# Gated mix of linear attention and a dilated local window: first tiles interleaved, warm-up on a constant, last columns split evenly

## The chip, the cores and the metric

The kernel runs on one core of a Trainium2 chip. The time is the device time of one execution in microseconds (us). The engines are TensorE (PE; its weight loads are shown as PEld), VectorE (DVE), ScalarE (ACT), GpSimd (POOL) and SyncE (SP), which issues most of the DMA transfers. A row named SPq or ACTq is the issue of a transfer on that engine's queue.

## The reference

```python
x = A_x                                    # [1, 2048, 1024] bf16
g = sigmoid((x * gate_w).sum(-1, keepdims=True))
# A: linear attention, 32 heads of 32
q, k, v = split(x @ A_wqkv)
pq, pk = phi(q), phi(k)                    # phi(t) = where(t > 0, t + 1, exp(t)) + 1e-6
kv = einsum("bhsd,bhse->bhde", pk, v);  z = einsum("bhsd->bhd", pk)
a = ((pq @ kv) / (pq . z + 1e-6)) @ A_wo
# B: each token attends to 8 keys, itself and every second token before it
q, k, v = split(x @ B_wqkv)
b = (softmax(q . k_window * 32**-0.5, masked at the start) @ v_window) @ B_wo
return g * a + (1 - g) * b                 # B_x is not used
```

## The kernel before

Activations are held transposed in `xT`: eight chunks of 128 features on the partitions, 2048 tokens along the free side. They arrive by 16 DMA transposes of 128 tokens each (`load_x`, line 1315). Even and odd tokens are separated, so a window of stride 2 becomes a run of neighbours. Weights arrive by `load_w` (line 1320) into slots of 1024 columns, in halves of 512 columns.

The stages stand one after the other on TensorE. (1) A warm-up: `WARM` small matmuls whose result is not used. (2) The values of B: for each block of four token tiles, half 0 and then half 1 of the 1024 value columns; every tile and half is one accumulation group of eight 128x512 matmuls (`group`, line 1340), copied out of PSUM by ACT or DVE (`move`, lines 1367 and 1368) into a ring `vst` and stored to `vB_hbm` (line 1389). (3) Keys and queries of B, with the window attention (`fill`) interleaved. (4) Keys of A, state, values and the fold of the output weights. (5) Queries of A and the output: for each tile two column ranges of 512, each the sum of 16 matmuls (line 1681), scaled by `gm` (line 1370) and stored (line 1688). The last tile is cut into (0, 512), (512, 896) and (896, 1024).

No engine's order is written by hand: `Prog.schedule` runs a list scheduler over all operations with estimated costs and priorities, chooses ACT or DVE for each `move`, and repeats the plan with PSUM banks chosen by when they were free in the plan before. What each engine executes is its own list in that order, with semaphore waits between the lists. Each queue issues its transfers in order.

For the first tiles this gives the following. On SP: x0, two pieces of the first weight half (chunks 4-5 and 6-7), x1, x2, x3, four pieces of the second half, then stores and x4 to x15. On ACT: the two other pieces of the first half (chunks 0-1 and 2-3), then the load of its function table. In the text these pieces are w0 to w3 (first half) and w4 to w7 (second half), and x0 to x15 are the token tiles. TensorE takes tile 0 in steps of two chunks, so that it waits for one weight piece at a time, and the other tiles in steps of eight:

```python
for t, half in [(4 * b + i, half) for b in range(NT // 4) for half in range(2) for i in range(4)]:
    ...
    step = 2 if t == 0 else 8
    for d in range(0, 8, step):
        o = group(bank, xs, w, [xr, ws[0].part((d, d + step), ...)], d, d + step)
```

The warm-up reads a tile `warm` that DVE sets to zero (line 1293). The same tile is used later for other purposes.

Of the kernel before, what the change touches and what calls it, by code (L numbers as in the profile page):

```python
# [9 lines left out]
BF16 = mybir.dt.bfloat16  # L10
# [1106 lines left out]
def build_kernel(nc, A_x, A_wqkv, A_wo, B_x, B_wqkv, B_wo, gate_w, out):  # L1117
    del B_x
    S = A_x.shape[1]
    NT = S // 128  # L1120
# [7 lines left out]
    def SB(shape, dtype, name, at=None):  # L1128
        n = SZ[dtype]
        for d in shape[1:]:  # L1130
            n *= d
        if at is None:
            at = base[0]
            base[0] += (n + 31) // 32 * 32
        uid[0] += 1
        h = nc.alloc_sbuf_tensor_at("%s_%d" % (name, uid[0]), list(shape), dtype, offset=at)
        return Tile("S", h, at, list(shape), dtype)
# [41 lines left out]
    banks = [Bank(i) for i in range(8)]  # L1179
# [4 lines left out]
    def hb(p0, p1, half):  # L1184
        return [("H%d" % half, p0, p1, None)]
# [4 lines left out]
    ws = [SB([128, 8, 1024], BF16, "w%d" % i) for i in range(4)]  # L1190
# [20 lines left out]
    warm = SB([128, 512], BF16, "warm")  # L1211
# [29 lines left out]
    FILL = 0.2  # L1241
    PVLAG = 3
    SUMS_AT = 2
    WARM = 46
    PASSES = 6
    mm = lambda n: max(n / 2400.0, 0.0267) + 0.0025
    act = lambda n: 0.19 + n / 1200.0
    dps = lambda n: 0.14 + n / 960.0

    def plan(seen):  # L1250

        P = Prog(nc, nc.alloc_semaphore)
# [23 lines left out]
        def C(eng, fn, cost, writes, reads=()):  # L1276
            return P.op(eng, fn, cost, reads=reads, writes=writes, prio=-1)
# [35 lines left out]
        def load_x(t, prio):  # L1313
            e_, r = t // 8, t % 8
            return P.op("sp", lambda e: e.dma_start_transpose(xT[:, :, t * 128:(t + 1) * 128], x2[e_, r * 128:(r + 1) * 128, :]),  # L1315
                        1.5, writes=[xT.part((0, 8), (t * 128, (t + 1) * 128))], prio=prio, chan="x%d" % t, lat=1.3)

        def load_w(slot, half, src, c0, prio, d0=0, d1=8, eng="sp", after=()):
            n = d1 - d0
            return P.op(eng, lambda e: e.dma_start(ws[slot][:, d0:d1, half * 512:half * 512 + 512], src[:, d0:d1, c0:c0 + 512]), 0.4 + 0.2 * n,  # L1320
                        writes=[ws[slot].part((d0, d1), (half * 512, half * 512 + 512))], prio=prio, chan="w%d_%d_%d" % (slot, half, d0), lat=0.55 * n, after=after)

        load_x(0, 0)
        load_w(0, 0, Bw, 2048, 0.1, 0, 2, "act")
        load_w(0, 0, Bw, 2048, 0.2, 2, 4, "act")
        load_w(0, 0, Bw, 2048, 0.3, 4, 6)
        load_w(0, 0, Bw, 2048, 0.4, 6, 8)
        for t in range(1, NT):
            load_x(t, 3 + t)
        for d in range(0, 8, 2):  # L1330
            load_w(0, 1, Bw, 2560, 6.1 + 0.1 * d, d, d + 2)
# [2 lines left out]
        main = Pool(banks[0:7])  # L1334

        def group(bank, lhs, rhs, reads, lo=0, hi=8):
            def fn(e):
                last = None
                for dc in range(lo, hi):
                    last = e.matmul(bank.ap(), lhs(dc), rhs(dc), start=(dc == 0), stop=(dc == 7))  # L1340
                return last
            return P.op("pe", fn, (hi - lo) * mm(512), reads=reads, writes=[bank.iv])
# [9 lines left out]
        def x_tile(t):  # L1352
            return (lambda dc: xT[:, dc, t * 128:(t + 1) * 128]), xT.part((0, 8), (t * 128, (t + 1) * 128))

        def x_chunk(u):
            return (lambda dc: xT[:, dc, u * 512:(u + 1) * 512]), xT.part((0, 8), (u * 512, (u + 1) * 512))

        def w_half(slot, half):
            return (lambda dc: ws[slot][:, dc, half * 512:half * 512 + 512]), ws[slot].part((0, 8), (half * 512, half * 512 + 512))

        def w_cols(slot, j):
            return (lambda dc: ws[slot][:, dc, j * 128:(j + 1) * 128]), ws[slot].part((0, 8), (j * 128, (j + 1) * 128))

        def move(dst, src, n, bank, reg, scale=None, reads=()):

            if scale is None:
                fd = lambda e: e.tensor_copy(dst, src())  # L1367
                fa = lambda e: e.activation(dst, src(), ACT.Copy)  # L1368
            else:
                fd = lambda e: e.tensor_scalar(dst, src(), scale, None, op0=ALU.mult)  # L1370
                fa = lambda e: e.activation(dst, src(), ACT.Copy, scale=scale)
            P.op("any", {"act": fa, "dve": fd}, {"act": act(n) + (0.1 if reads else 0.0), "dve": dps(n)}, reads=[bank.iv] + list(reads), writes=[reg])

        for i in range(WARM):
            P.op("pe", lambda e: e.matmul(banks[7].ap(0, 156), warm[:, 0:128], warm[:, 0:156], start=True, stop=True), 0.13, reads=[warm.all()], writes=[banks[7].iv], prio=-1)


        early = {(2, 0): (1, 0, Bw, 1024, 21), (4, 1): (2, 0, Bw, 0, 22), (7, 1): (1, 1, Bw, 1536, 23), (10, 1): (2, 1, Bw, 512, 24),
                 (12, 1): (3, 0, Aw, 1024, 25), (14, 1): (3, 1, Aw, 1536, 26)}
        for t, half in [(4 * b + i, half) for b in range(NT // 4) for half in range(2) for i in range(4)]:  # L1380
            vt, vs = vst.next()
            xs, xr = x_tile(t)
            bank = main.next()
            w, wr = w_half(0, half)
            step = 2 if t == 0 else 8
            for d in range(0, 8, step):
                o = group(bank, xs, w, [xr, ws[0].part((d, d + step), (half * 512, half * 512 + 512))], d, d + step)
            move(vt[:, :], bank.ap, 512, bank, vt.all())
            P.op("sp", lambda e, t=t, vt=vt, half=half: e.dma_start(vB_hbm[t * 128:(t + 1) * 128, half * 512:half * 512 + 512], vt[:, :]), 0.6, reads=[vt.all()],
                 writes=[hb(t * 128, (t + 1) * 128, half)], chan="vst%d" % vs, lat=0.5, prio=5)  # L1390
            if (t, half) in early:
                load_w(*early[t, half], after=[o])
# [14 lines left out]
        main = Pool(banks[0:4])  # L1407
# [77 lines left out]
        for e_ in range(2):  # L1485
            if True:
                for j in range(8):
                    for isq in range(2):
                        for u in (2 * e_, 2 * e_ + 1):
                            bank = main.next()  # L1490
                            w, wr = w_cols(1 + isq, j)
                            xs, xr = x_chunk(u)
# [45 lines left out]
        for t in range(NT):  # L1538
            xs, xr = x_tile(t)
            for r in range(2):  # L1540
                bank = main.next()
                w, wr = w_half(3, r)
                o = group(bank, xs, w, [xr, wr])
# [33 lines left out]
        main = Pool(banks[0:3])  # L1577
# [23 lines left out]
        for c in range(8):  # L1601
            tl = xns[c // 2]
            cs = (c % 2) * 128
            for r in range(2):
                bank = main.next()
# [63 lines left out]
        def output(t):  # L1669
            o_, os_ = osb.next()  # L1670
            e_, r = t // 8, t % 8
            parts = [(0, 512), (512, 1024)] if t < NT - 1 else [(0, 512), (512, 896), (896, 1024)]
            for f0, f1 in parts:
                bank = main.next()
                n = f1 - f0

                tt = (t * 128, (t + 1) * 128)
                for lh, w, first in ((qT, ws[0], True), (aT, ws[5], False)):
                    def fn(e, bank=bank, f0=f0, f1=f1, lh=lh, w=w, first=first):
                        for k in range(8):  # L1680
                            last = e.matmul(bank.ap(0, f1 - f0), lh[:, k, t * 128:(t + 1) * 128], w[:, k, f0:f1], start=(first and k == 0), stop=(not first and k == 7))  # L1681
                        return last
                    P.op("pe", fn, 8 * mm(n), reads=[lh.part((0, 8), tt), w.part((0, 8), (f0, f1))], writes=[bank.iv])
                move(o_[:, f0:f1], lambda bank=bank, n=n: bank.ap(0, n), n, bank, o_.part((f0, f1)), gm[:, t:t + 1], [gm.all()])
                P.ops[-1].late = t == NT - 1
                if t == NT - 1 or f1 == 1024:
                    c = f0 if t == NT - 1 else 0
                    P.op("sp", lambda e, c=c, f1=f1: e.dma_start(out2[e_, r * 128:(r + 1) * 128, c:f1], o_[:, c:f1]), 0.5,
                         reads=[o_.part((c, f1))], chan="out%d_%d" % (os_ + 2 * (t == NT - 1), c), lat=1.0, name="out")
                    P.ops[-1].late = t == NT - 1  # L1690
# [10 lines left out]
        main = Pool(banks)  # L1701
# [17 lines left out]
        for t in range(NT):  # L1719
            if t + 2 < NT:  # L1720
                scaled(t + 2)
            output(t)
            if t + 5 < NT:
                queries(t + 5)

        C("act", lambda e: e.preload_act_table_set("natural_log_exp_and_others"), 1.3, [])
        P.ops[-1].prio = 2.5
        P.schedule()
        return P, flag_op, [max(o.end for o in P.held[n]) for n in range(len(takes))]

# [2 lines left out]
    for _ in range(PASSES):  # L1733
        got = plan(seen)
        seen = got[2]
        if best is None or got[0].span < best[0].span:
            best = got
    P, flag_op = best[:2]
# [40 lines left out]
def bass_gated_mix__linear_attn_block__sliding_local_dilated__prompt_kernel(nc, A_x, A_wqkv, A_wo, B_x, B_wqkv, B_wo, gate_w, out):  # L1779
    return build_kernel(nc, A_x, A_wqkv, A_wo, B_x, B_wqkv, B_wo, gate_w, out)  # L1780
# [28 lines left out]
```

## Time and profile before

| | |
|---|---|
| median of 3 runs | 489.4 us (488.79 to 491.67) |
| the profiled execution | 488.05 us, its span 486.3 us |
| granted TensorE clock, mean | 1.000 |
| busy: PE, DVE, ACT, POOL | 474.2, 290.3, 148.1, 40.9 us |
| moved by DMA | 47.72 MB, mean 98 GB/s |

The span runs from the first to the last instruction of the core. Busy time of an engine counts its instructions; a matmul's row includes its way through the array, so rows of one stream overlap. Queue rows give the time of the issue; the landing of a transfer is given apart, from issue to the last byte. An entry in brackets at the end of a row is the idle time of the engine before it and what ended it.

### The profile page before, as it was taken

The page shows a single profiled execution, that of the slowest core. Times are in us where ns is not written, and L with a number is a line of the kernel's source. Part 1 is how long each engine was busy: PE and PEld are TensorE (multiplying, and loading weights), DVE is VectorE, ACT ScalarE, POOL GpSimd, SP SyncE. Part 2 cuts the span into 40 slices and gives each one's busy share as a digit, 9 for nine tenths or more (in the row PEclk, how much of TensorE's full clock was granted, in tenths as well). Part 3 has the DMA queues.
Part 4 walks back from the last instruction along what each step waited for, and adds up shares of the span by engine and source line. Part 5 has one row for each costly group of instructions (what it writes and reads, how often), then busy time and mean ns, then how long its engine had stood idle before and what let it go on. Part 6 is the DMA issues. An engine that isn't in the chain of part 4 may idle for free.

```text
span 486.3 us, 10903 instructions
## 1 busy us (share of the span) xinstructions
PE 474.2 (97%) x4820; PEld 228.6 (47%) x4883; DVE 290.3 (60%) x486; ACT 148.1 (30%) x231; POOL 40.9 (8%) x43
## 2 busy tenths in 40 slices
PE   8999999999999999999999999999999999999997
PEld 6444444444444444444455545444444444444443
DVE  2121455899777777766733222289987777767522
ACT  2111121112344444766554356544222000011000
POOL 3000000000000000000025657100000000000000
PEclk9999999999999999999999999999999999999999
DMA  8999997224000032213004430252233111122111
GB/s 223 205 204 281 341 332 232 86 88 129 3 23 25 27 115 58 35 34 111 24 25 121 141 91 4 89 174 41 54 80 87 44 43 44 44 71 60 44 44 48
DMA packets 71833, 47.72 MB, mean 98 GB/s; under 512 B 36449, under 2 KB 65378, under 8 KB 71778
## 3 DMA queue, kind: packets, MB, share of 16 engines
q1 hardware_dynamic: 71234, 46.42, 34.7%
q8 instruction: 40, 0.66, 0.6%
q10 hardware_dynamic: 544, 0.52, 0.4%
q14 instruction: 15, 0.12, 0.1%
HBM read 30.15 MB, written 8.39 MB: 79 GB/s over the span
## 4 chain that ended last, share of the span: by engine, by line
PE 94%; SPq 2%; issue 2%; DMA 1%; DVE 0%; ACT 0%
PE ps_all L1340 54%; PE ps_all L1681 23%; PE ps_all L1609 11%; PE ps_all L1426 2%; PE ps_all L1446 2%; SPq L1315 1%; DMA w<-in_B_wqkv_dram 1%; PE ps_all L1452 1%; SPq L1320 1%; PE ps_all L1588 1%; PE ps_all L1636 0%; DVE qT L1463 0%; ACT L L1461 0%; PE ps_all L1558 0%; ACT L L1462 0%
## 5 line engine op out<-in xcount | busy, mean ns | idle before, releaser
L1340 PE MATMUL ps_all<-w,xT 128*128 128x512 bf16 x493 | 109.9, 379 | 2.6 <-issue 2.1
L1340 PE MATMUL ps_all<-xT,w 128*128 128x512 bf16 x498 | 109.9, 379 | 1.7 <-issue 1.4
L1340 PEld LDWEIGHTS ps_all<-xT,w 128*128 128x128 bf16 x512 | 49.4, 98 | 58.6
L1340 PEld LDWEIGHTS ps_all<-w,xT 128*128 128x128 bf16 x512 | 48.8, 98 | 58.3 <-DMA w<-in_B_wqkv_dram 0.7
L1346 ACT ACTIVATE e<-ps_all 128x512 bf16<-128x512 f32 x64 | 38.0, 598 | 109.7 <-PE ps_all L1340 107.9
L1681 PE MATMUL ps_all<-kT,aT 128*128 128x512 bf16 (+2 forms) x261 | 60.3, 373 | 0.2
L1681 PE MATMUL ps_all<-w,qT 128*128 128x512 bf16 (+2 forms) x259 | 60.2, 372 | 0.3
L1340 PE MATMUL ps_all<-kT,xT 128*128 128x512 bf16 x248 | 57.1, 379 | 0.6 <-issue 0.3
L1609 PE MATMUL ps_all<-pk,xn 128*128 128x512 bf16 x243 | 54.9, 379 | 2.0 <-issue 1.9
L1681 PEld LDWEIGHTS ps_all<-w,qT 128*128 128x128 bf16 x264 | 25.6, 98 | 30.0
L1681 PEld LDWEIGHTS ps_all<-kT,aT 128*128 128x128 bf16 x264 | 25.4, 98 | 29.8 <-issue 0.2
L1340 PEld LDWEIGHTS ps_all<-kT,xT 128*128 128x128 bf16 x256 | 24.7, 98 | 30.0 <-issue 0.5
L1463 DVE TENSOR_TENSOR qT<-ps_all,L 128x456 bf16<-128x456 f32 (+1 forms) x36 | 21.1, 625 | 27.6 <-ACT L L1462 27.6
L1609 PEld LDWEIGHTS ps_all<-pk,xn 128*128 128x128 bf16 x256 | 24.1, 98 | 27.6
L1367 DVE CAST vst<-ps_all 128x512 bf16<-128x512 f32 x15 | 10.4, 692 | 44.4 <-PE ps_all L1340 44.4
L1370 DVE TENSOR_SCALAR o<-ps_all,gm 128x512 bf16<-128x512 f32 (+2 forms) x27 | 19.7, 731 | 28.0 <-PE ps_all L1681 28.0
L1435 DVE TENSOR_TENSOR E<-E,msk 128x1824 bf16<-128x1824 bf16 (+1 forms) x18 | 20.4, 1133 | 26.5 <-ACT E L1432 26.5
L1432 ACT ACTIVATE E<-ps_all 128x1824 bf16<-128x1824 f32 (+1 forms) x18 | 30.4, 1688 | 14.3 <-PE ps_all L1426 13.6
L1347 DVE TENSOR_SCALAR e<-e 128x512 bf16<-128x512 bf16 x64 | 18.4, 288 | 27.2 <-ACT e L1346 27.2
L1571 POOL TENSOR_TENSOR zacc<-zacc,pk 128x1024 f32<-128x1024 f32 x15 | 31.9, 2130 | 16.6 <-DVE E L1435 15.8
L1301 DVE TENSOR_TENSOR mx<-mx,kT 128x1024 bf16<-128x1024 bf16 x32 | 20.8, 686 | 6.9 <-ACT kT L1368 6.8
L1368 ACT ACTIVATE vst<-ps_all 128x512 bf16<-128x512 f32 x17 | 10.2, 597 | 48.0 <-PE ps_all L1340 45.1
(67 smaller groups left out, 354.4 us busy)
## 6 DMA issues: line engine op xcount, KB each, us to landing
v<-vB_hbm SPq DMA_DIRECT2D x36, 128.0 KB, 2.7
vB_hbm<-vst SPq DMA_DIRECT2D x32, 128.0 KB, 6.1
w<-in_B_wqkv_dram SPq DMA_DIRECT2D x4, 1024.0 KB, 8.7
xt<-in_A_x_dram SPq DMA_DIRECT2D x16, 256.0 KB, 4.9
w<-in_A_wqkv_dram SPq DMA_DIRECT2D x4, 1024.0 KB, 10.1
xn<-in_A_x_dram SPq DMA_DIRECT2D x8, 512.0 KB, 3.7
out_dram<-o SPq DMA_DIRECT2D x15, 256.0 KB, 2.1
kT<-in_A_wqkv_dram SPq DMA_DIRECT2D x2, 1024.0 KB, 5.6
```

The costliest lines, as they stand in the source:

```text
L1301: P.op("dve", lambda e, m=m, op=op: e.tensor_tensor(m[:, 0:n], m[:, 0:n], src, op), 0.08 + n / 1920.0, reads=[m.all(), reg], writes=[m.all()],
L1340: last = e.matmul(bank.ap(), lhs(dc), rhs(dc), start=(dc == 0), stop=(dc == 7))
L1346: P.op("act", lambda e: e.activation(e_[:, :], bank.ap(), ACT.Exp), act(512), reads=[bank.iv], writes=[e_.all()])
L1347: P.op("dve", lambda e: e.tensor_scalar(e_[:, :], e_[:, :], 1.0, 1e-6, op0=ALU.min, op1=ALU.add), 0.25, reads=[e_.all()], writes=[e_.all()])
L1367: fd = lambda e: e.tensor_copy(dst, src())
L1370: fd = lambda e: e.tensor_scalar(dst, src(), scale, None, op0=ALU.mult)
L1432: P.op("act", lambda e: e.activation(E[:, 0:32 * nq].rearrange("p (j q) -> p j q", j=4), ps[:, 4:8, 0:8 * nq], ACT.Exp), act(32 * nq), rea ...
L1435: mk = P.op("dve", lambda e: e.tensor_tensor(ev(), ev(), m[:, :, :].rearrange("p r q -> p (r q)")[:, None, :].to_broadcast([128, 16, 2 * n ...
L1463: P.op("dve", lambda e, L=L, pb=pb, g=g: e.tensor_tensor(qT[:, 4 * g:4 * g + 4, t0 + qs:t0 + qs + 2 * nq].rearrange("p c (h q) -> p h c q" ...
L1571: P.op("pool", lambda e, t=t: e.tensor_tensor(zacc[:, :], zacc[:, :], pkS[:, t, :], ALU.add), 2.2, reads=[src, zacc.all()], writes=[zacc.a ...
L1609: last = e.matmul(bank.ap(), tl[:, t, cs:cs + 128], pkS[:, t, r * 512:(r + 1) * 512], start=(t == 0), stop=(t == NT - 1))
L1681: last = e.matmul(bank.ap(0, f1 - f0), lh[:, k, t * 128:(t + 1) * 128], w[:, k, f0:f1], start=(first and k == 0), stop=(not first and k == 7))
```

## The change

- `WARM` goes from 46 to 34, and the warm-up matmuls read a constant 1.0 that the framework keeps in SBUF (broadcast over 128 and 156 columns) in place of the tile `warm`; they wait for nothing.
- ACT's table load is put at the head of ACT's list, ahead of its two weight pieces. Before it stood behind them.
- x1 is issued directly after x0, ahead of SP's two pieces of the first half.
- In the first block, tiles 0 and 1 are interleaved by weight piece: in half 0 four chunks of tile 0, four of tile 1, then two and two, two and two; in half 1 two and two for each of the four pieces. Two accumulation groups are open in two PSUM banks. Tiles 2 and 3 and the other blocks are as before.
- The last tile's second half is cut into 256 and 256 columns in place of 384 and 128.

```diff
-    WARM = 46
+    WARM = 34
...
+        P.op("act", lambda e: e.preload_act_table_set("natural_log_exp_and_others"), 1.3, [], prio=-1)
         load_x(0, 0)
+        load_x(1, 0.1)
         load_w(0, 0, Bw, 2048, 0.1, 0, 2, "act")
         load_w(0, 0, Bw, 2048, 0.2, 2, 4, "act")
         load_w(0, 0, Bw, 2048, 0.3, 4, 6)
         load_w(0, 0, Bw, 2048, 0.4, 6, 8)
-        for t in range(1, NT):
+        for t in range(2, NT):
             load_x(t, 3 + t)
...
+        one = lambda n: nc.const_aps.tensor(1.0, [128, n], BF16)
         for i in range(WARM):
-            P.op("pe", lambda e: e.matmul(banks[7].ap(0, 156), warm[:, 0:128], warm[:, 0:156], start=True, stop=True), 0.13, reads=[warm.all()], writes=[banks[7].iv], prio=-1)
+            P.op("pe", lambda e: e.matmul(banks[7].ap(0, 156), one(128), one(156), start=True, stop=True), 0.13, writes=[banks[7].iv], prio=-1)
...
-        for t, half in [(4 * b + i, half) for b in range(NT // 4) for half in range(2) for i in range(4)]:
+        steps = []
+        for b in range(NT // 4):
+            for half in range(2):
+                if b == 0:
+                    cuts = [(0, 4), (4, 6), (6, 8)] if half == 0 else [(0, 2), (2, 4), (4, 6), (6, 8)]
+                    steps += [[(i, half, lo, hi) for i in range(2)] for lo, hi in cuts]
+                    steps += [[(2, half, 0, 8)], [(3, half, 0, 8)]]
+                else:
+                    steps += [[(4 * b + i, half, 0, 8)] for i in range(4)]
+        open_ = {}
+        for t, half, lo, hi in [p for q in steps for p in q]:
+            xs, xr = x_tile(t)
+            if lo == 0:
+                open_[t, half] = main.next()
+            bank = open_[t, half]
+            w, wr = w_half(0, half)
+            o = group(bank, xs, w, [xr, ws[0].part((lo, hi), (half * 512, half * 512 + 512))], lo, hi)
+            if hi < 8:
+                continue
             vt, vs = vst.next()
-            xs, xr = x_tile(t)
-            bank = main.next()
-            w, wr = w_half(0, half)
-            step = 2 if t == 0 else 8
-            for d in range(0, 8, step):
-                o = group(bank, xs, w, [xr, ws[0].part((d, d + step), (half * 512, half * 512 + 512))], d, d + step)
             move(vt[:, :], bank.ap, 512, bank, vt.all())
...
-            parts = [(0, 512), (512, 1024)] if t < NT - 1 else [(0, 512), (512, 896), (896, 1024)]
+            parts = [(0, 512), (512, 1024)] if t < NT - 1 else [(0, 512), (512, 768), (768, 1024)]
...
-        C("act", lambda e: e.preload_act_table_set("natural_log_exp_and_others"), 1.3, [])
-        P.ops[-1].prio = 2.5
```

## The prediction

> **What bounds the kernel now.** First I read the page's busy shares and its chain of work that ended last:
>
> ```profile
> PE 474.2 (97%) x4820; PEld 228.6 (47%) x4883; DVE 290.3 (60%) x486; ACT 148.1 (30%) x231; POOL 40.9 (8%) x43
> ...
> PE 94%; SPq 2%; issue 2%; DMA 1%; DVE 0%; ACT 0%
> ```
>
> TensorE is busy for 97% of the span and carries 94% of the chain, so only an edit that moves TensorE's first matmul, a hole between its matmuls, or the few microseconds after its last one can move the end. The change touches the first stretch and the last. The timeline of the first (start, length, engine, line; then idle time and what ended it):
>
> ```profile
> 0.80 0.94 ACTq L1320 DMA_DIRECT2D w<-in_B_wqkv_dram  x2
> 0.80 1.35 SPq L1315 DMA_TRANSPOSE xT<-in_A_x_dram  x1
> ...
> 0.93 0.27 DVE L1293 MEMSET warm<- 128x256 uint32 x1 [0.93 <-PEq L1794]
> 1.25 5.26 PE L1375 MATMUL ps_all<-warm 128*128 128x156 bf16 x46 [1.25 <-DVE warm L1293]
> 1.77 1.28 ACT L1726 ACT_TABLE_LOAD   x1 [1.77 <-PEq L1794]
> 2.21 1.07 SPq L1320 DMA_DIRECT2D w<-in_B_wqkv_dram  x2
> 3.33 4.98 SPq L1315 DMA_TRANSPOSE xT<-in_A_x_dram  x3
> 6.35 8.45 PE L1340 MATMUL ps_all<-w,xT 128*128 128x512 bf16 x37
> 8.15 6.16 PEld L1340 LDWEIGHTS ps_all<-w,xT 128*128 128x128 bf16 x30 [0.40 <-DMA xT<-in_A_x_dram]
> 15.06 30.18 PE L1340 MATMUL ps_all<-w,xT 128*128 128x512 bf16 x136 [0.26 <-DMA w<-in_B_wqkv_dram]
> ...
> 19.33 1.23 SPq L1315 DMA_TRANSPOSE xT<-in_A_x_dram  x1
> ```
>
> The 46 warm-up matmuls wait for a memset (0.93 to 1.20) and run from 1.25 to 6.51 with the tails of the last ones; real work starts at 6.35. The weight loader waits once for a transposed token tile (8.15, 0.40 us), and TensorE once for a weight piece (15.06, with 0.26 us of idle shown). That hole is larger than it looks, since a matmul's row includes its pipeline. Eight 512-column matmuls follow one another in 477.69 − 475.96 = 1.73 us (rows in the tail below), so one takes 0.216 us. In program order 38 matmuls stand before the one that waits at 15.06: four tiles of 8 in the first half, then six of tile 0's second half. From 6.35 they would need 38 × 0.216 = 8.21 us, to 14.56; so 0.50 us is lost in all. I use an "effective start": the time at which an unbroken stream would have begun to be where it is after the last hole. Now it is 15.06 − 8.21 = **6.85**. After that the row shows 30 us without a wait.
>
> When do the data land? The view of a tile's transfers gives issue time and issue-to-landing, for x0, then x1, x2 and all sixteen; for the weight pieces w0 and w1 together (ACT's queue), w2 and w3 together (SP's); and the chain for the last piece of the second half, w7:
>
> ```profile
> L1315 SPq DMA_TRANSPOSE xT<-in_A_x_dram x1: 1350/1350/1350, 0.8 to 0.8; - x1
> DMA to landing us min/median/max: 5.1/5.1/5.1
> ...
> L1315 SPq DMA_TRANSPOSE xT<-in_A_x_dram x1: 1239/1239/1239, 3.3 to 3.3; - x1
> DMA to landing us min/median/max: 4.8/4.8/4.8
> ...
> L1315 SPq DMA_TRANSPOSE xT<-in_A_x_dram x1: 2348/2348/2348, 4.6 to 4.6; - x1
> DMA to landing us min/median/max: 4.6/4.6/4.6
> ...
> L1315 SPq DMA_TRANSPOSE xT<-in_A_x_dram x16: 1231/1284/2436, 0.8 to 35.8; - x16
> ...
> DMA to landing us min/median/max: 3.3/3.9/5.9
> ```
>
> ```profile
> L1320 ACTq DMA_DIRECT2D w<-in_B_wqkv_dram x2: 423/456/488, 0.8 to 1.3; - x2
> DMA to landing us min/median/max: 2.8/3.6/4.4
> ...
> L1320 SPq DMA_DIRECT2D w<-in_B_wqkv_dram x2: 457/510/562, 2.2 to 2.8; - x2
> DMA to landing us min/median/max: 4.4/4.4/4.5
> ```
>
> ```profile
> 10.00 5.01 DMA w<-in_B_wqkv_dram
> ```
>
> So x0 lands at 0.80 + 5.1 = 5.9, w1 at 1.3 + 4.4 = 5.7, w2 and w3 at 2.2 + 4.4 = 6.6 and 2.8 + 4.5 = 7.3, x1 at 3.3 + 4.8 = 8.1, x2 at 4.6 + 4.6 = 9.2, w7 at 15.0. Landings follow the order of issue.
>
> **The change, part by part.** *Second tile's load up, tiles interleaved.* SP now issues x0, x1, w2, w3, x2, x3, then w4 to w7 and x4: the same six issues stand ahead of x2, so x2 and what follows keep their times. x1's issue takes 1.24 us (4.98 for three in the row, the first starting at 3.33, x2 at 4.6), so x1 moves from 3.3 to about 2.2, and w2, w3 from 2.2, 2.8 to about 3.5, 4.1. TensorE does four matmuls of tile 0 (which now wait for x0, w0 and w1 together), four of tile 1, then two and two for w2, two and two for w3, tiles 2 and 3 whole; in the second half two and two per piece. Each arrival sets a lower bound on the effective start, landing minus matmuls ahead × 0.216:
>
> x0 5.9 − 0 = 5.9. w1 5.7 − 0 = 5.7. x1 (2.2 + 5.0, between the 5.1 and 4.8 of x0 and x1) 7.2 − 4 × 0.216 = 6.35. w2 3.5 + 4.4 = 7.9 − 8 × 0.216 = 6.2. w3 4.1 + 4.5 = 8.6 − 12 × 0.216 = 6.0. x2 9.2 − 16 × 0.216 = 5.75. w7 15.0 − 44 × 0.216 = 5.5.
>
> The largest is x1's, 6.35, so 6.85 − 6.35 = **0.5 us gained**. The hole at w7 goes because six more matmuls stand before it (44, not 38); what is late next is x1, a hole of about 0.4 us after the first four matmuls. Bounds: if x1, w2 and w3 land sooner than issue times say, x0 at 5.9 remains, a gain of 0.95; if x1 still lands at 8.1, the start is 8.1 − 0.86 = 7.24, a loss of 0.4.
>
> *Table load first.* ACT now begins with the table load (1.28 us at 1.77) and only then issues w0 and w1, which tile 0 waits for; x0 and x1 are behind SP and not touched. The trace never shows a DMA issue behind a running ACT instruction, so the cost is bounded by 0 (the issue goes out while the table loads) and 1.28 us (it waits). In the second case w1 lands at 5.7 + 1.28 = 7.0, and the start is 7.0 instead of 6.35, 0.65 us worse. I take 0: issue (ACTq) and execution (ACT) are separate rows in this view, and of the two ends nothing shows the second. On ACT's own side the load is covered, since the first eviction comes after 8 us.
>
> *Warm-ups: 34 on a constant.* The constant is set before the engines enter the block, so they start near 0.8 (where ACT and SP start), 0.45 us sooner, and are 12 fewer. The record of the warm-ups, and two windows of 0.2 us (PE busy and matmuls in flight come first, the granted clock third from the end):
>
> ```profile
> L1375 PE MATMUL ps_all<-warm x46: 228/336/336, 1.3 to 6.3; 128*128 128x156 bf16 x46
> ```
>
> ```profile
> 5.00:5.20 0.20, 0.20 (x4) 0.20 (x3) 0.00 (x0) 0.00 (x0) 0.20 (x2) 1.00 1.28 366
> 6.00:6.20 0.20, 0.20 (x6) 0.20 (x4) 0.00 (x0) 0.00 (x0) 0.00 (x0) 1.00 1.16 369
> ```
>
> With lengths from 336 to 228 ns and 4 then 6 in flight per 0.2 us window, spacing goes from (0.336 + 0.2) / 4 = 0.134 to (0.228 + 0.2) / 6 = 0.071 us between 5.2 and 6.0, though the granted clock reads 1.00 in both. About 4.2 us of continuous work came before the faster rate. Thirty-four at the slow rate take 4.56 us, to about 5.4, just past that point (0.8 + 4.2 = 5.0); then TensorE idles until 5.9. I charge nothing: both the twelve removed and the earlier end lie ahead of x0's landing. If that cover fails, because the faster rate has not come by then, every real matmul costs 0.216 × 0.134 / 0.071 = 0.41 instead of 0.216 us until it does (second rival).
>
> The Trainium skill, "TensorE: Matmul & The Clock Gate" (Part 1: The HAM clock gate), says that the array runs at half rate until one busy window of about 3.4 us has passed, and that this window runs freely, so the moment shifts from run to run. The 4.2 us above agrees with it; by that rule, as an estimate, a stretch of 4.56 us need not hold a whole window, which speaks against the shorter warm-up.
>
> *Other orders.* Many evictions of the first 100 us change between ACT and DVE, and the queues of stores and token loads are reshuffled. TensorE's own order after the first four tiles is unchanged. The cover is the distance of the loads: x7 is issued at 19.33 with 13 loads and 4 stores ahead, as many as after the change; it lands within 5.9 us, by 25.2 at worst and by the median 3.9 at 23.2, and is needed after 88 matmuls, 6.35 + 19.0 = 25.35. Without that cover each microsecond late is one lost. I take 0.
>
> *Last columns 256 and 256.*
>
> ```profile
> 475.96 1.89 PE L1681 MATMUL ps_all<-w,qT 128*128 128x512 bf16 x8
> 477.69 1.89 PE L1681 MATMUL ps_all<-kT,aT 128*128 128x512 bf16 x8
> 479.41 1.46 PE L1681 MATMUL ps_all<-w,qT 128*128 128x384 bf16 x8
> 482.01 0.61 PE L1681 MATMUL ps_all<-w,qT 128*128 128x128 bf16 x8
> 482.22 0.62 DVE L1370 TENSOR_SCALAR o<-ps_all,gm 128x384 bf16<-128x384 f32 x1 [1.61 <-PE ps_all L1681]
> 482.46 0.61 PE L1681 MATMUL ps_all<-kT,aT 128*128 128x128 bf16 x8
> ```
>
> ```profile
> 482.86 1.84 SPq L1688 DMA_DIRECT2D out_dram<-o  x2
> 483.11 0.35 DVE L1370 TENSOR_SCALAR o<-ps_all,gm 128x128 bf16<-128x128 f32 x1 [0.28 <-PE ps_all L1681]
> ```
>
> ```profile
> out_dram<-o SPq DMA_DIRECT2D x1, 128.0 KB, 1.7
> out_dram<-o SPq DMA_DIRECT2D x1, 96.0 KB, 2.6
> out_dram<-o SPq DMA_DIRECT2D x1, 32.0 KB, 2.3
> ```
>
> Sixteen matmuls of 384 columns take 482.01 − 479.41 = 2.60 us, sixteen of 128 take 2 × 0.45 = 0.90; 256 lies midway, 32 × 0.109 = 3.5, no change. A matmul's own length is its eight's less seven spacings: 1.46 − 7 × 0.1625 = 0.32 at 384 columns, 0.61 − 7 × 0.056 = 0.22 at 128, so the last one at 256 ends some 0.05 later. The last eviction goes from 0.35 to the mean of 0.35 and 0.62, +0.135. The last store, issued now when the eviction ends (483.46) and landing 2.3 later at 485.8, is issued 0.19 us later. A store of 64 KB isn't in the trace: 2.6 for 96 KB, 2.3 for 32, 1.7 for 128. I take 2.0, between its neighbour in size below and the best, since its predecessor is now over a microsecond away instead of 0.6. Sum +0.19 − 0.3 = **−0.1 us**, bounds −0.4 and +0.5.
>
> The Trainium skill, "DMA: Bandwidth & Descriptors" (Specifications), puts the least size for line rate at 512 B; rows of 128 columns are 256 B, rows of 256 are 512 B. That would favour 1.7, though the 96 KB store with 768 B rows took 2.6 here.
>
> **Sum.** −0.5 − 0.1 = −0.6 us on the profiled execution's 488.05 (span 486.3 and 1.75 around it), 487.45. The runs' median of 489.4 is 1.35 above that execution; on that footing the forecast is **488.8 us**, a gain of 0.1%. One per cent (4.9 us) is about what a measurement of this kernel can tell from no change.
>
> **Rivals.** *The table load holds w0 and w1* (the change doesn't start sooner as it says). Effective start 7.0 against 6.85: +0.15 − 0.1, 489.45. For it: one queue, in order. Against: separate rows for issue and execution.
>
> *Slower: the real matmuls begin at the slow rate.* Place: the gap between the last warm-up (5.4) and x0 (5.9). It decides when the faster rate has not come by 5.4; then another 4.2 us at 0.41 us hold about 10 matmuls instead of 19. Started at 5.9, ten are done at 10.1, an effective start of 10.1 − 2.16 = 7.95, +1.1 − 0.1: 490.4. With w1 held too it starts at 7.0 and reaches 9.05: 491.5. For it: 4.56 us of warm-up is hardly more than the 4.2 that it took. Against: the gap is short, and the rate rose before the end here. The clock-gate section of the Trainium skill's page "TensorE: Matmul & The Clock Gate" describes this mechanism.
>
> *All six first transfers land together.* If moving x1 only reorders one saturated stream, x1 lands at 8.1: 7.24, +0.4 − 0.1, 489.7. For it: the same bytes move in the same time. Against: landings followed issue.
>
> **How the numbers follow.** Forecast 0.5, held queue 0.18, slow rate 0.2, together 0.12. The range starts from the best bounds, 489.4 − 0.95 − 0.4 = 488.05, less 1.25 because a median can come out like the profiled execution (1.35 lower): 486.8. Above, it reaches 491.2, through the slow-rate case and most of its worse form. The forecast's own range is 487.4 to 489.9. Every case lies within 1% of 489.4; I leave 0.03 each side for late loads and stray effects.
>
> **What would show it.** Right: warm-ups from 0.8 ending near 5.2; the first real matmul near 5.9; a wait for x1 after four of them; no hole at a second-half weight piece; tile 4 about 0.5 us sooner; the last store landing 2.0 us or less after its issue. Wrong: ACTq issues at 2.1; real matmuls 0.41 us apart after 6; a hole at x5 to x7; a difference over 2 us anywhere else.

## The result and the profile after

The changed kernel took 488.03 us (median of 22 runs, 486.66 to 490.36); the kernel before took 489.81 us beside it (22 runs, 488.55 to 493.31). The ratio is 0.9962, with a 95% interval of 0.9948 to 0.9976: 1.9 us faster, at least 1.2 and at most 2.5. The profiled execution took 487.48 us with a span of 485.7 us, 0.57 and 0.6 us less than the profiled execution before. So the profiled pair shows the 0.6 us that was forecast, while the medians show three times as much. In a second comparison the ratio was 0.9975 (0.9954 to 0.9996).

The page after, busy shares and the chain that ended last:

```profile
PE 473.4 (97%) x4808; PEld 228.6 (47%) x4871; DVE 291.0 (60%) x487; ACT 147.4 (30%) x230; POOL 40.8 (8%) x43
...
PE 96%; issue 2%; DMA 1%; DVE 0%; ACT 0%
```

TensorE's share is as before. In the chain it has gone from 94% to 96%, because the transfers and issues that stood in it at the start have left it. The timeline of the start shows why:

```profile
0.80 1.28 ACT L1323 ACT_TABLE_LOAD   x1 [0.80 <-PEq L1807]
0.80 2.71 SPq L1315 DMA_TRANSPOSE xT<-in_A_x_dram  x2
...
0.83 0.96 ACTq L1320 DMA_DIRECT2D w<-in_B_wqkv_dram  x2
0.84 4.58 PE L1378 MATMUL ps_all<-const-bfloat16-1.0 128*128 128x156 bf16 x34 [0.84 <-PEq L1807]
...
3.57 1.09 SPq L1320 DMA_DIRECT2D w<-in_B_wqkv_dram  x2
...
6.09 24.08 PE L1342 MATMUL ps_all<-w,xT 128*128 128x512 bf16 x108 [0.67 <-DMA xT<-in_A_x_dram]
```

Four things are to be seen. ACT issues its two weight pieces (ACTq, 0.83) while the table load runs (0.80 to 2.08). The 34 warm-up matmuls start at 0.84, last to 5.42 and are followed by 0.67 us of idle time, ended by x0. The first real matmul starts at 6.09, and there is no further wait in the row: neither at x1 nor at a second-half piece. x1's landing is the other number (issue and landing of x0 and x1 together):

```profile
L1315 SPq DMA_TRANSPOSE xT<-in_A_x_dram x2: 1309/1330/1350, 0.8 to 2.2; - x2
DMA to landing us min/median/max: 4.3/4.7/5.2
```

x1 was issued at 2.2 and landed 4.3 us later, at 6.5, not 7.2. What this start is worth is read at a point behind it in the same order of TensorE, the first matmuls of the first window attention. Their row before, and after:

```profile
126.10 0.70 PE L1426 MATMUL ps_all<-qT,kT 32*64 32x57 bf16 x64
```

```profile
125.50 0.70 PE L1441 MATMUL ps_all<-qT,kT 32*64 32x57 bf16 x64
```

That is 0.60 us sooner. The end of the span, with the last two evictions and the last store:

```profile
481.14 0.48 DVE L1372 TENSOR_SCALAR o<-ps_all,gm 128x256 bf16<-128x256 f32 x1 [0.50 <-PE ps_all L1696]
...
482.88 0.48 DVE L1372 TENSOR_SCALAR o<-ps_all,gm 128x256 bf16<-128x256 f32 x1 [1.26 <-PE ps_all L1696]
```

```profile
L1703 SPq DMA_DIRECT2D out_dram<-o x1: 332/332/332, 483.4 to 483.4; - x1
DMA to landing us min/median/max: 1.8/1.8/1.8
```

The last eviction starts 0.23 us sooner than before (483.11), the store lands 1.8 us after its issue where it took 2.3, and the span ends 2.82 us after that eviction began, where it ended 3.19 us after it, 0.37 us less. Between the start and the tail, 0.37 us was given back at one place, near 195 us. The `E,v` rows are matmuls of the attention's second half; the rows behind them (ACT's logarithm, and an issue of SP) wait for these matmuls. The kernel before comes first, with an earlier attention for comparison:

```profile
180.02 0.51 PE L1446 MATMUL ps_all<-E,v 64*32 64x57 bf16 x40
180.61 0.99 ACT L1461 ACTIVATE L<-ps_all 128x456 f32<-128x456 f32 x2 [1.90 <-PE ps_all L1446]
...
191.95 0.51 PE L1446 MATMUL ps_all<-E,v 64*32 64x57 bf16 x40
...
195.13 0.45 SPq L1419 DMA_DIRECT2D v<-vB_hbm  x1
195.14 0.99 ACT L1461 ACTIVATE L<-ps_all 128x456 f32<-128x456 f32 x2 [2.77 <-PE ps_all L1340]
```

```profile
191.35 0.51 PE L1461 MATMUL ps_all<-E,v 64*32 64x57 bf16 x40
...
195.09 0.45 SPq L1434 DMA_DIRECT2D v<-vB_hbm  x1
195.09 0.99 ACT L1476 ACTIVATE L<-ps_all 128x456 f32<-128x456 f32 x2 [3.33 <-PE ps_all L1342]
```

Normally ACT's logarithm starts 0.1 us after those matmuls (180.53 and 180.61). Here it starts 2.7 and 3.2 us after them, in both kernels at 195.1, together with an issue of SP that waits for the same matmuls. The next attention matmuls wait for it. TensorE arrived there 0.6 us sooner, and nearly two thirds of that was waited away. The pair's difference of 0.60 us is thus 0.60 from the start and 0.37 from the tail, less these 0.37; that it equals the forecast is luck.

### The profile page after: what moved, and what is told of

Same layout as the page of the kernel before. It is cut to its first block, busy times and chain, and to the rows that moved or that the text cites. A ratio compares the mean times of both kernels' runs of the same rounds, so it can differ in the third digit from the quotient of the medians.

```text
span 485.7 us, 10878 instructions
## 1 busy us (share of the span) xinstructions
PE 473.4 (97%) x4808; PEld 228.6 (47%) x4871; DVE 291.0 (60%) x487; ACT 147.4 (30%) x230; POOL 40.8 (8%) x43
## 4 chain that ended last, share of the span: by engine, by line
PE 96%; issue 2%; DMA 1%; DVE 0%; ACT 0%
PE ps_all L1342 56%; PE ps_all L1696 23%; PE ps_all L1624 11%; PE ps_all L1441 2%; PE ps_all L1461 2%; DMA xT<-in_A_x_dram 1%; PE ps_all L1467 1%; PE ps_all L1603 1%; PE ps_all L1651 0%; DVE qT L1478 0%; ACT L L1476 0%; PE ps_all L1573 0%; DVE o L1372 0%; ACT L L1477 0%; PE ps_all L1596 0%
## 5 line engine op out<-in xcount | busy, mean ns | idle before, releaser
L1696 PE MATMUL ps_all<-kT,aT 128*128 128x512 bf16 (+1 forms) x261 | 60.3, 373 | 0.2
L1696 PE MATMUL ps_all<-w,qT 128*128 128x512 bf16 (+1 forms) x259 | 60.2, 372 | 0.3
L1372 DVE TENSOR_SCALAR o<-ps_all,gm 128x512 bf16<-128x512 f32 (+1 forms) x27 | 19.7, 731 | 28.1 <-PE ps_all L1696 28.1
L1369 DVE CAST kT<-ps_all 128x512 bf16<-128x512 f32 x25 | 17.1, 690 | 11.7 <-PE ps_all L1342 10.9
```

## Experiments

Two readings serve for every trace: the start of the first window attention ("start"), and the time from the start of the last eviction to the end of the span ("tail"). Runs of one kernel spread over 2 to 5 us, so the comparisons of times resolve 0.5 to 1.3 us; most verdicts rest on the traces, one for each kernel.

**Shorter warm-up alone.**

```diff
-    WARM = 46
+    WARM = 34
```

> The kernel before with 34 warm-up matmuls instead of 46 and nothing else. Theory W (the profiled execution of before was a lucky one: usually the faster rate does not come during the warm-up, so 46 at 0.134 us from 1.25 end at 7.4 and hold the first real matmul there): the start is set by x0 (5.9) and the hole at w7 remains (effective start 6.85), so 0.5 us faster than before, near 489.3. Theory P (the profiled execution is typical, warm-up ends at 6.35): the earlier start only makes the hole at w7 longer, 0.0 us. Theory S (the shorter warm-up leaves the real matmuls at the slow rate): 0.5 to 1 us slower. In the trace: first real matmul at 6.0, a hole of about 0.9 us before the w7 matmul.

488.43 us, ratio 0.9989 (0.9976 to 1.0003), that is −0.5 us with 0 inside the interval. The timeline of its start:

```profile
1.25 4.60 PE L1375 MATMUL ps_all<-warm 128*128 128x156 bf16 x34 [1.25 <-DVE warm L1293]
6.00 2.00 PE L1340 MATMUL ps_all<-w,xT 128*128 128x512 bf16 x8
...
15.14 14.79 PEld L1340 LDWEIGHTS ps_all<-w,xT 128*128 128x128 bf16 x70 [0.62 <-DMA w<-in_B_wqkv_dram]
```

The first real matmul starts at 6.00 instead of 6.35, and the hole at w7 (15.14) is still there. The first window attention begins at 126.18, as before (126.10). Theory P's reading fits: a stream that waits for w7 gains nothing from an earlier beginning. Nor did 0.5 to 1 us of slow matmuls appear.

**Last columns alone.**

```diff
-            parts = [(0, 512), (512, 1024)] if t < NT - 1 else [(0, 512), (512, 896), (896, 1024)]
+            parts = [(0, 512), (512, 1024)] if t < NT - 1 else [(0, 512), (512, 768), (768, 1024)]
```

> The kernel before with the last columns cut 256 and 256 and nothing else. If the tail of the changed kernel's trace (last store issued at +0.17, landing 1.8 instead of 2.3 us after it) is typical: 0.35 us faster, near 489.45. If a store's landing is chance: 0 to 0.2 slower. Nothing before the last tile may move.

488.26 us, ratio 0.9991 (0.9981 to 1.0002): −0.45 us, again with 0 inside the interval. The last store:

```profile
L1688 SPq DMA_DIRECT2D out_dram<-o x1: 332/332/332, 483.3 to 483.3; - x1
DMA to landing us min/median/max: 1.9/1.9/1.9
```

Tail 2.97 us against 3.19. This gain in the trace needs nothing of the start.

**Interleaving and x1 alone.** The loads and the loop over steps of the change, with the rest as before.

```diff
         load_x(0, 0)
+        load_x(1, 0.1)
...
-        for t in range(1, NT):
+        for t in range(2, NT):
...
+                    steps += [[(i, half, lo, hi) for i in range(2)] for lo, hi in cuts]
```

> The kernel before with x1 moved up and tiles 0 and 1 interleaved; warm-up (46, zero tile), table load and last columns as before. Theory P: effective start 6.35 as the x1 bound says, 0.5 us faster, near 489.3. Theory W: the warm-up holds the start at 7.4 with or without it, 0.0 us; in a trace in which the faster rate comes early it would show the 0.5.

488.13 us, ratio 0.9989 (0.9979 to 1.0000): −0.55 us. Its start:

```profile
1.25 5.11 PE L1376 MATMUL ps_all<-warm 128*128 128x156 bf16 x46 [1.25 <-DVE warm L1293]
...
6.20 24.12 PE L1341 MATMUL ps_all<-w,xT 128*128 128x512 bf16 x111
```

No hole behind 6.20, and the first window attention begins at 125.43, 0.67 us sooner than before. The interleaving thus brings the start's gain by itself, with the old warm-up. But the first real matmul is not bound by x0 here. x0 in this trace:

```profile
L1315 SPq DMA_TRANSPOSE xT<-in_A_x_dram x1: 1347/1347/1347, 0.8 to 0.8; - x1
...
DMA to landing us min/median/max: 4.8/4.8/4.8
```

x0 had landed at 5.6, and the first real matmul starts only at 6.20, without idle time behind the warm-ups: here the 46 from 1.25 hold it. In the old order this goes unseen, because w7 holds the stream anyway: in the kernel before, x0 lands at 5.9 and the first real matmul starts at 6.35. The last store of its 384 and 128 columns landed 2.9 us after its issue, tail 3.68.

**The changed kernel with 46 warm-up matmuls**, run twice.

```diff
-    WARM = 34
+    WARM = 46
```

> The changed kernel with 46 warm-up matmuls on the constant instead of 34. Theory W: from 0.84 at 0.134 us they end at 7.0, an effective start of 7.0 instead of 6.25, 0.75 us slower than the changed kernel, 1.0 faster than before: near 488.8. Theory P: the faster rate comes near 5.0, they end at 6.1 and cost nothing: as the changed kernel, near 488.0.

487.29 us, ratio to before 0.9968 (0.9957 to 0.9978), −1.6 us. Theory W, by which the warm-up holds the start, falls for the warm-up on the constant: the first real matmul starts at 6.06, with 0.27 us of idle time ended by x0. The old warm-up, which starts 0.41 us later, did hold the first real matmul (at 6.20 to 6.62, with x0 landed at 5.6 to 5.9) in four of the seven traces that have it.

> The changed kernel with 46 warm-up matmuls on the constant. If the 34 of the changed kernel end before the faster rate comes and the first real matmuls pay for it (two traces: 34 at the slow rate throughout): 0.2 us faster than the changed kernel; if 46 at the slow rate hold the start in other executions (0.84 + 6.2 = 7.0): up to 0.7 slower.

487.99 us, ratio 0.9959 (0.9936 to 0.9983). The changed kernel itself, on that chip:

> The changed kernel unchanged, on the chip and beside the runs of before that the next kernel has. By the steps shown so far (start 0.6 to 0.85, last store 0.65): 1.3 us faster than before. If the 1.9 us of the first comparison are real: 1.9. In the trace: first real matmul at 6.0 to 6.1, no hole at a second-half piece, last store landing 1.6 to 1.9 after its issue.

487.68 us, ratio 0.9975 (0.9954 to 0.9996), that is −1.2 us; the interval holds both 1.3 and 1.9. Its start:

```profile
0.84 4.54 PE L1378 MATMUL ps_all<-const-bfloat16-1.0 128*128 128x156 bf16 x34 [0.84 <-PEq L1807]
5.96 24.33 PE L1342 MATMUL ps_all<-w,xT 128*128 128x512 bf16 x112 [0.57 <-DMA xT<-in_A_x_dram]
```

The first window attention begins at 125.19, against 125.50 in the first trace of the same kernel, and at 125.29 and 125.31 with 46. The two can't be told apart; twelve warm-up matmuls more or less are worth nothing that these runs resolve, and no version here is shown to beat the changed kernel.

**No warm-up.**

```diff
-    WARM = 34
+    WARM = 0
```

> The changed kernel with no warm-up at all: the real matmuls begin at the slow rate. Theory of the slow rate as a price per matmul: x0 lands at 6.0, the first matmuls are 0.41 us apart for about 4.2 us, so the effective start is near 8.0 instead of 6.25: 1.8 us slower than the changed kernel, as before or 0.2 slower. Rival (arrivals, not the rate, set this stretch): the slow matmuls hide in the waits for data, under 0.5 us slower than the changed kernel.

490.19 us, ratio 1.0012 (0.9991 to 1.0033), some 2.2 us slower than the changed kernel by the medians of the two comparisons. The weight loads show the spacing of the matmuls:

```profile
5.89 24.43 PE L1342 MATMUL ps_all<-w,xT 128*128 128x512 bf16 x102 [5.89 <-DMA xT<-in_A_x_dram]
6.28 0.15 PEld L1342 LDWEIGHTS ps_all<-w,xT 128*128 128x128 bf16 x1 [0.28 <-issue]
6.70 0.15 PEld L1342 LDWEIGHTS ps_all<-w,xT 128*128 128x128 bf16 x1 [0.28 <-issue]
...
10.12 0.15 PEld L1342 LDWEIGHTS ps_all<-w,xT 128*128 128x128 bf16 x1 [0.28 <-issue]
10.52 19.52 PEld L1342 LDWEIGHTS ps_all<-w,xT 128*128 128x128 bf16 x91 [0.26 <-issue]
```

Eleven matmuls are up to 0.427 us apart, until 10.5, and then the even stream begins. The first window attention begins at 127.38, 1.9 us later than in the changed kernel's first trace. So the second rival's mechanism exists and its price was nearly right (10 matmuls, about 4.2 us); the changed kernel only brushes it, in that first trace, where all 34 ran at the slow rate and the first real matmul was followed after 0.38 us. The rule of the Trainium skill, "TensorE: Matmul & The Clock Gate" (Part 1: The HAM clock gate), that a busy stretch of some 3.4 us with a free-running phase opens the full rate, agrees with 4.6 us here (5.89 to 10.5) and 4.2 us in the kernel before. Over all fourteen traces the full rate comes 2.7 to 5.7 us after TensorE's first matmul; the shortest, with the store on ACT's queue, is less than the Trainium skill's 3.4, and there the measurement decides.

**What makes the last store land late?** Five kernels. First, the 384-column store on another queue:

```diff
-                    P.op("sp", ...
+                    P.op("act" if f1 == 896 else "sp", ...
```

> The kernel before, but the store of the 384 columns is issued by ACT's queue instead of SP's. In the traces so far the 128-column store lands 2.3 to 3.3 us after its issue and the 256-column one 1.6 to 1.9. Theory Q (the last store stands in SP's queue behind a 384-column store issued 0.6 us earlier that itself lands 2.6 to 3.3 after its issue): alone in its queue the 128-column store lands 1.6 to 1.9 after its issue; if the 384-column one still takes 3 us from ACT, that one now ends the span, at about +0.1 of before. Theory R (rows of 256 B are slow to store): the 128-column store still takes 2.3 or more.

489.06 us, ratio 1.0008 (0.9989 to 1.0026). The two stores:

```profile
L1688 ACTq DMA_DIRECT2D out_dram<-o x1: 365/365/365, 483.2 to 483.2; - x1
DMA to landing us min/median/max: 3.1/3.1/3.1
```

```profile
L1688 SPq DMA_DIRECT2D out_dram<-o x1: 332/332/332, 483.8 to 483.8; - x1
DMA to landing us min/median/max: 2.6/2.6/2.6
```

Alone in SP's queue, the 128-column store still takes 2.6 us: theory Q, in which it stands behind its neighbour in the queue, falls. Next, the cut turned round:

```diff
-            parts = ... [(0, 512), (512, 896), (896, 1024)]
+            parts = ... [(0, 512), (512, 640), (640, 1024)]
```

> The kernel before with the last columns cut 128 and then 384. The store before the last is out 1.9 us ahead of it (16 matmuls of 384 columns, 2.6 us, less the evictions) and the last has rows of 768 B. Theory Q: the last lands 1.6 to 1.9 after its issue; the eviction of 384 columns is 0.27 longer than that of 128, so the tail (last eviction to end of span) is 0.3 to 0.6 us shorter than 3.2 to 3.7, less 0.27: 0.1 to 0.4 us faster than before. Theory R: likewise for the last store (no 256 B rows at the end); so Q and R agree here, and differ only on the 128-column store in the middle, which by R takes longest.

488.43 us, ratio 0.9987 (0.9969 to 1.0005). The two stores ahead of the last (512 and 128 columns, issued at 480.5 and 480.9), then the last:

```profile
L1688 SPq DMA_DIRECT2D out_dram<-o x2: 335/376/417, 480.5 to 480.9; - x2
DMA to landing us min/median/max: 3.6/3.7/3.8
```

```profile
L1688 SPq DMA_DIRECT2D out_dram<-o x1: 332/332/332, 483.3 to 483.3; - x1
DMA to landing us min/median/max: 1.6/1.6/1.6
```

The last lands after 1.6, tail 2.72, but both others took over 3.5: the 512-column store too, which took 1.7 in all the kernels shown so far. One piece of 512 columns:

```diff
-            parts = ... [(0, 512), (512, 896), (896, 1024)]
+            parts = ... [(0, 512), (512, 1024)]
```

> The kernel before with the last 512 columns as one piece: one store of 128 KB, its predecessor 3.4 us ahead. Theories Q and R: it lands 1.7 us after its issue as the 512-column stores before it do; the eviction is 0.75 instead of 0.35, the last matmul ends about 0.16 later; tail from the last eviction's start 0.75 + 0.05 + 1.7 + 0.5 = 3.0, against 3.2 to 3.7: the same as to 0.4 us faster than before, 0.2 us slower than the 256 and 256 cut.

488.92 us, ratio 0.9995 (0.9977 to 1.0013). Its last store lands 1.7 us after its issue, tail 2.93, as expected; the longer eviction uses up most of what the landing gains. Then the short runs, put into the changed kernel:

```diff
+                wv = warm[:, :].rearrange("p (h c) -> p h c", h=2)[:, :, 0:128]
...
+                    move(wv, lambda ...: bank.ap(0, n).rearrange("p (h c) -> p h c", h=2), ...)
```

> The changed kernel, with the last 256 columns evicted into a tile with a gap after 128 columns, so that the last store of 64 KB is made of runs of 256 B on the SBUF side; its time of issue is that of the changed kernel. Theory R (short runs are slow to store): it lands 2.3 us or more after its issue instead of 1.6 to 1.9, and the tail from the last eviction's start grows from 2.8 to 3.3 or more. Theory Q2 (the last store is slow when another was issued 0.6 us before it, on whichever queue): 1.6 to 1.9, no change.

487.51 us, ratio 0.9953 (0.9929 to 0.9976). The last store:

```profile
L1708 SPq DMA_DIRECT2D out_dram<-warm x1: 389/389/389, 483.6 to 483.6; - x1
DMA to landing us min/median/max: 1.8/1.8/1.8
```

Still 1.8, tail 2.77: theory R, by which runs of 256 B are slow, falls as far as the SBUF side goes. Last, two stores close together:

```diff
+                ends = [(0, f1)] if t < NT - 1 else [(f0, f1)] if f0 == 0 else [(512, 768), (768, 1024)]
+                for c, f1 in ends if t == NT - 1 or f1 == 1024 else []:
```

> The kernel before with the last 512 columns as one accumulation and one eviction, but stored as two stores of 256 columns issued one right after the other (about 0.4 us). Theory Q2: the second lands 2.3 or more after its issue. Theory R (runs of 512 B): 1.6 to 1.9, so the tail from the last eviction's start is 0.75 + 0.05 + 0.4 + 1.8 + 0.5 = 3.5.

489.31 us, ratio 0.9992 (0.9964 to 1.0019). The pair:

```profile
L1688 SPq DMA_DIRECT2D out_dram<-o x2: 332/378/425, 483.8 to 484.2; - x2
DMA to landing us min/median/max: 1.6/1.6/1.7
```

Issued 0.4 us apart, they took 1.6 and 1.7: closeness alone (theory Q2) doesn't make a store late either.

All three theories of the late store fall. First the pattern. In the 384 and 128 cut the last store lands 2.3, 2.7, 2.9 and 2.6 us after its issue (four traces: before, shorter warm-up, interleaving, ACT's queue), and the tail is 3.19 to 3.68, mean 3.50. In the 256 and 256 cut it lands in 1.6 to 1.9 (seven traces), tail 2.57 to 2.97, mean 2.78. In both cuts the store ahead of the last is slow, 2.6 to 3.3 and 3.1 to 3.5 us, and the last lands 0.2 us after it (0.4 in the kernel before).

The traces show what the slow stores have in common. The transfers in the stretch of the last two stores of the shorter warm-up's trace (482.7 to 486.5), and in the stretch of the store that goes ahead of the pair in the last kernel (480.4 to 483.0):

```profile
q8 instruction: 1, 0.02, 1.9%
...
out_dram<-o SPq DMA_DIRECT2D x1, 96.0 KB, 3.1
out_dram<-o SPq DMA_DIRECT2D x1, 32.0 KB, 2.7
```

```profile
q8 instruction: 1, 0.02, 2.8%
...
out_dram<-o SPq DMA_DIRECT2D x1, 128.0 KB, 2.5
```

Besides the stores there is one packet of 16 KB, of the kind that the profile calls instruction (the program's own instructions being loaded, by that name). Every trace has one near the end; it takes 0.9 to 1.6 us. Each store has sixteen reports in the trace, one for each of its parts, and counts as landed at the last. Of the stores of the last tile, fifteen parts report 1.4 to 1.7 us after the issue whatever the size (32 to 128 KB), and in the slow ones a single part comes later. (The exception is the last store of the kernel before, whose issue alone took 1.21 us.) In thirteen of fourteen traces the late part's packets start within 0.02 us of the end of the 16 KB packet. So one part of a store stands behind it. The pair at the very end is quick because in that kernel the 16 KB packet came early, at 480.6 to 481.8, and made the store ahead slow (2.5). The 128-column stores, with rows of 256 B on the HBM side, have fifteen parts done after 1.44 us where their issue took its usual time, so these rows aren't slow either.

This also tells what the cut did. In the eleven traces of the two cuts the last store lands 1.25 to 1.51 us after the end of the 16 KB packet, nine of them within 1.25 to 1.30. With 384 and 128 columns the packet ends 1.2 to 1.9 us after the last eviction begins, with 256 and 256 only 0.8 to 1.2. No run moved the packet by itself, and what sets its moment wasn't tried.

## Why the prediction was right, and where its terms were off

- *Sign and size.* Forecast 488.8 us, −0.6; measured 488.03, −1.9 (−2.5 to −1.2). The direction and the range hold; the likeliest gain was too small by a factor of three. The comparison told 0.4% from no change, where the prediction took one per cent for the limit.
- *Base.* The sum was made on a profiled execution of 488.05 us that is quicker than all 22 later runs of the kernel before (lowest 488.55). Its last store (2.3 us) was the quickest of the four traces with that cut. Adding 1.35 us put the level right, but a difference taken from one lucky execution stays too small.
- *Tail, forecast −0.1 (bounds −0.4 and +0.5).* This is the term that was mis-sized. The means of the tails differ by **0.72 us**, outside the bounds; the last eviction begins 3.7 us after the first matmul of the last 512 columns in both cuts. The eviction's part was right (0.35 to 0.48, +0.13, and no change in TensorE's 3.5 us). The landing was set at 2.0 against 2.3; it is 1.6 to 1.9 against 2.3 to 2.9. The reason given for it, the size of the store and the distance to its predecessor, isn't what the traces show: it is where the 16 KB packet falls, a term that the sum didn't have. That the sign came out right is luck in this part. The Trainium skill, "DMA: Bandwidth & Descriptors" (Specifications), whose least size for line rate is 512 B, pointed the same way; but these traces show no slowness of 256 B rows.
- *Start, forecast −0.5, by x1.* Seven traces with the old order of the first tiles (among them those of the shorter warm-up, the cuts and the stores) reach the first window attention at 125.66 to 126.23, mean 126.02; six with the new one and a warm-up at 125.19 to 125.50, mean 125.33: **−0.69 us**. The step that was off is x1's landing, taken 5.0 us after its issue from x0's and x1's rows; it took 4.1 to 4.4. So in the changed kernel x0 is the bound, with the first real matmul at 5.96 to 6.09; the prediction had this as its limit of 0.95. The hole at w7 went as the count of 44 matmuls said.
- *Table load, taken as 0.* Right, and shown by a row: ACT's issues stand at 0.83 beside the running load. The first rival falls.
- *Warm-up, taken as 0.* Right for the kernel before, where w7 sets the stream, and between 34 and 46 on the constant (first real matmul at 5.96 to 6.09). Not quite right for the interleaved tiles: there the old warm-up held the start at 6.20. By the prediction's own bounds the next one in that trace would have been x2: landed at 9.35, less 16 × 0.216, plus the 0.14 us that x0 shows from landing to matmul, is 6.03. So this cost some 0.2 us, an estimate from one trace. The slow-rate rival is a real mechanism, seen here in full only without a warm-up; between 0 and 34 nothing was tried. The clock of 1.00 that the prediction read at 5.0 is no measurement: the trace's record of the clock begins at 5.41, when the rate rises.
- *All six transfers together.* Falls: x1 landed at 6.5, ahead of w2 (3.6 + 3.8 = 7.4). That landings follow the order of issue holds on SP's queue alone; in the prediction's own figures w1, issued at 1.3 by ACT, lands at 5.7, ahead of x0, issued at 0.8 (5.9).
- *Other orders, taken as 0.* No hole at x5 to x7. But the wait near 195 us takes part of the gain back in some executions. Beyond the regular 11.93 us from one attention to the next, it cost 0 to 1.46 us in seven traces with the old order (mean 0.47) and 0.15 to 2.15 in seven with the new one (mean 0.94). These overlap, so that the new order pays more there is a guess; that the wait differs from execution to execution is shown, and it is part of the spread of the runs.
- *The sum.* Start 0.69 and tail 0.72 make 1.41 us; this lies within both measured intervals. What of the rest of 1.9 is real stays open.

## What to carry to other kernels

Read a term that is as small as a landing time from several traces before building a difference on it: one execution had the best of four. When a stream waits at two places, only the last wait sets the gain: here the earlier first matmul alone gave nothing, and putting more matmuls ahead of the late piece gave nearly all of it. At the end of a kernel, ask what else the DMA engines carry while the last stores are out: here one packet of instructions decided when the last store landed; its size and its queue did not.

## What the runs showed of the hardware

- TensorE's matmuls of 512 columns run 0.427 us apart instead of 0.216 for the first eleven without a warm-up. The profile's granted clock doesn't tell of it: its record begins only when the rate rises (at 5.41 in the kernel before, at 10.48 without a warm-up), and the stretches ahead of it are printed as 1.00.
- A queue of ACT issues transfers while a table load runs on ACT (0.83 to 1.79 beside 0.80 to 2.08).
- One 16 KB packet of instructions, 0.9 to 1.6 us long, delays one of the sixteen parts of a store. Clear of it, stores of 64 to 128 KB landed 1.6 or 1.7 us after their issue; with it, stores of 32 to 128 KB took up to 3.8.
- Near 195 us a release by TensorE reaches ACT and SP 2.4 to 4.6 us late in every trace, and 0.1 us after the matmuls one attention earlier. A store of 384 maxima (1.5 KB) is issued some 10 us ahead of it; whether it is the cause was not tried.
